# Copies, unit order and warm-up at the start of a hashed attention with a maxout FFN on one Trainium2 core

## The chip, the cores and the metric

The kernel runs on one NeuronCore of a Trainium2 chip. The core has TensorE (PE, matrix products; PEld is its loading of weights), VectorE (DVE), ScalarE (ACT), GpSimd (POOL) and SyncE (SP). The last three also issue DMAs here. The metric is the device time of one execution in microseconds, lower is better. The kernel before took 299.92 us, the median of three runs (297.75 to 301.09).

## The reference

Attention over 4 batches, 8 heads, 768 positions, 64 dimensions. A query sees only the keys of its own hash bucket, six bits from the signs of a projection. The output goes through a maxout layer.

```python
q_bits = (einsum('bhsd,dk->bhsk', q, proj) > 0)      # 6 bits; k_bits alike
mask   = q_bucket[:, :, :, None] == k_bucket[:, :, None, :]
scores = where(mask, scale * q @ k.T, -1e9)
attn   = exp(scores - max); attn = attn / (sum(attn) + 1e-9)
x      = (attn @ v) as (3072, 512)
h      = maximum(maximum(x @ w1, x @ w2), x @ w3)     # 512 -> 768
out    = h @ w_out                                    # 768 -> 512
```

## The kernel before

Heads are worked in 16 pairs. For each pair q and k are loaded as they lie, transposed on TensorE (`tgroup`, L150: one side and one head each, three transposes) and copied out of PSUM to the fp32 tile `T2` (L158, L160). The tile `S` is what the scores read: per side, head and position parity it has 64 rows of data in bf16 and six rows of hash bits as plus or minus one half, so that one product of 70 rows gives score and bit agreement together. `S` is filled from three sides:

- the even copy (`even`, L217): GpSimd copies the lower 64 rows of `T2`, both sides and heads at once
- the odd copies (`odd`, L221): one for k, one for q, from the upper 64 rows; pair 1 has them on VectorE, pairs 8 to 15 on ScalarE; in pairs 2 to 7 the transposes' own step writes the odd rows straight from PSUM (L166, L168)
- the hash (`hashes`, L205): four products with the projection, VectorE makes bits of their signs (L208), and four small DMAs put them into `S` (L214); in pair 1 head 0's two are issued by SyncE, head 1's two by GpSimd

Pair 0 has a start of its own with finer steps (L191, L196).

The unit of work is one pair, one half of the queries (384), two key blocks and one head: 12 units a pair, 192 in all. A unit is two score products (L304) and one exp on ScalarE (L307) into one of 14 `AT` tiles; there are two PSUM buffers for scores. `units` says in which order the key blocks and heads of a half come: by key blocks (both heads of a block, then the next block), or by head (three blocks of head 0, then three of head 1).

The order of all instructions is written out by one loop over the units, and each engine works its own in that order. In iteration u the loop issues, in this order: weight loads at fixed units (on GpSimd), the scores of unit u+1, due steps of the normalization, one waiting late step (`late`), then in some slots either a transpose group of a later pair or, once four groups are through, its hash (`do_hash`). The first group of a pair also issues the loads of q and k of the pair two ahead, on GpSimd. `do_hash` runs the steps that the pair wants in front of the hash, then the hash, and puts those for behind it on `late`, from which one is taken in each iteration.

When a half is complete, `values` multiplies it with v (L328, 24 products) and sums its rows (L342, 12 products), VectorE takes both out of PSUM (L350 to L353), and the reciprocal goes by a DMA round trip (L374 to L388). In some halves the first 16 of the 24 value products come earlier, at slot 4 of the half's six units (`values_part`), since by key blocks the first four chunks of both heads are then there. From unit 61 on, the FFN of the batch before (L246 to L276) fills TensorE between the units; the last batch's FFN is the end of the kernel.

Ahead of everything, TensorE multiplies a tile of zeros several times (L400), while the first loads are on their way.

The loop's lines about the late step and the early values part:

```python
            if late:
                late.pop(0)()
            slot = u % UPG                       # UPG = 6, UPP = 12
            ...
            if slot == 4 and UPP < u < PAIRS_AT: # PAIRS_AT = 60
                values_part(*units[u][0:2], 0, EARLY_CH)
```

Of the kernel before, what the change touches and what calls it, by code (L numbers as in the profile page):

```python
# [17 lines left out]
def kernel(  # L18
# [37 lines left out]
    ODD_LATE, ODD_PSUM = 1, 8  # L56
# [29 lines left out]
    def load_proj():  # L86
        for par in range(2):
            rows = slice(par * D, (par + 1) * D)
            nc.scalar.dma_start(pst[rows, :], proj[:, :])
            nc.vector.tensor_copy(pj[rows, 1 + par, 0:NBITS], pst[rows, :])  # L90
            nc.vector.tensor_copy(pj[rows, 0, par : 2 * NBITS : 2], pst[rows, :])
# [17 lines left out]
    def load(pi, eng):  # L109
        b, jj = divmod(pi, HPAIR)  # L110
        nats = [nat.tile([P, 2, NCH * D], FP32, tag=nm, name=nm) for nm in ("qnat", "knat")]
        for h0, nh in ((0, 1), (1, 1)) if pi == 0 else ((0, 2),):
            for side in (1, 0):
                h = 2 * jj + h0
                eng.dma_start(nats[side][:, h0 : h0 + nh, :],
                                  (q, k)[side][b, h : h + nh].rearrange("h (p c) d -> p h (c d)", p=P))
        natural[pi] = nats

    def load_v(pi, eng):
        b, jj = divmod(pi, HPAIR)  # L120
        vn = vpool.tile([P, 2, NCH * D], FP32, tag="vnat", name="vnat")
        eng.dma_start(vn[:], v[b, 2 * jj : 2 * jj + 2].rearrange("h (p c) d -> p h (c d)", p=P))
        vo = vopool.tile([P, 2, NCH * D], FP16, tag="vo", name="vo")
        vones[pi] = vo
        return lambda: nc.gpsimd.tensor_copy(vo[:], vn[:])
# [7 lines left out]
    def prep_groups(pi):  # L133
        st = {}

        def begin():
            st["T2"] = t2pool.tile([P, 2, 2, HALF], FP32, tag="T2", name="T2")
            st["S"] = spool.tile([KR, 2, 2, 2, HALF], BF16, tag="S", name="S")
            trans[pi] = st["S"]
            if 2 < pi + 2 < NPAIR:  # L140
                load(pi + 2, nc.gpsimd)

        def tgroup(side, hd):
            def go():
                if not st:
                    begin()
                mp = ms_ps.tile([P, 512], FP32, tag="ms", name="mp")
                n = natural[pi][side]
                for i in range(CH2):
                    nc.tensor.transpose(mp[:, i * P : (i + 1) * P], n[:, hd, 2 * i * D : (2 * i + 2) * D], iden[:])  # L150
                o = st["T2"][:, side, hd, :]
                if pi == 0 and (hd, side) != (0, 1):
                    if side == 0:
                        nc.scalar.mul(o, mp[:, 0:HALF], QS)
                    else:
                        nc.scalar.copy(o, mp[:, 0:HALF])
                elif side == 0:
                    nc.vector.tensor_scalar(out=o, in0=mp[:, 0:HALF], scalar1=QS, scalar2=None, op0=AluOp.mult)  # L158
                else:
                    nc.vector.tensor_copy(o, mp[:, 0:HALF])  # L160
                if pi == 0:
                    nc.gpsimd.tensor_copy(st["S"][0:D, side, hd, 0, :], o[0:D])
                elif ODD_LATE < pi < ODD_PSUM:
                    o, i_ = st["S"][0:D, side, hd, 1, :], mp[D : 2 * D, 0:HALF]
                    if side == 0:
                        nc.vector.tensor_scalar(out=o, in0=i_, scalar1=QS, scalar2=None, op0=AluOp.mult)  # L166
                    else:
                        nc.vector.tensor_copy(o, i_)  # L168
            return go
# [49 lines left out]
        def odd(side):  # L219
            copy = nc.scalar.copy if pi > ODD_LATE else nc.vector.tensor_copy  # L220
            return lambda: copy(st["S"][0:D, side, :, 1, :], st["T2"][D : 2 * D, side])  # L221
# [7 lines left out]
                    lambda: bits_first(1, early[2:]), lambda: bits_first(0, ((0, 1, 0, HALF),)),  # L229
                    lambda: bits_first(1, ((0, 1, 0, HALF),))]  # L230
        odds = [odd(1), odd(0)]
        if pi == ODD_LATE:
            return [tgroup(s, h) for h in (0, 1) for s in (1, 0)], hashes, odds + [even], []
        return [tgroup(s, h) for h in (0, 1) for s in (1, 0)], hashes, [even], odds if pi >= ODD_PSUM else []

    def ffn_groups(b):
        xb = xts[b]
# [44 lines left out]
    units = []  # L282
    for pi in range(NPAIR):
        for qh in range(2):
            inner = [(kp, hd) for kp in range(NCH // 2) for hd in range(2)]
            units += [(pi, qh, kp, hd) for kp, hd in (sorted(inner, key=lambda e: e[1]) if pi == 0 else inner)]
    unit_of = {e: u for u, e in enumerate(units)}
    NU = len(units)
    UPB = NU // B
    UPG = NCH  # L290
    UPP = 2 * UPG
# [4 lines left out]
    PAIRS_AT = UPB + UPP  # L296
# [12 lines left out]
    def do_hash():  # L309
        if hash_ready:  # L310
            hs, hv, odds = hash_ready.pop(0)
            for g in odds:
                g()
            hs()
            late.extend(hv)
# [80 lines left out]

    with tc.manual_schedule():
        wm = ms_ps.tile([P, 512], FP32, tag="ms", name="wm")
        for _ in range(9):
            nc.tensor.matmul(wm[:], warm[:, 0:P], warm[:], start=True, stop=True)  # L400
        load(0, nc.sync)
        load_proj()
        load(1, nc.sync)
        cast_v = {0: load_v(0, nc.sync)}
        load(2, nc.sync)
        first = prep_groups(0)
        for g in first:
            g()

        prep, hash_ready, late, ffn, steps = [], [], [], [], []  # L410
        f_credit = 0.0
        for p2 in range(1, NPAIR):
            ts, *hs = prep_groups(p2)
            prep += [(p2, i, g, hs) for i, g in enumerate(ts)]
        for u in range(NU):
            pi = units[u][0]
            b, ub = divmod(u, UPB)
            if u % UPP == 0 and pi + 1 < NPAIR:
                cast_v[pi + 1] = load_v(pi + 1, nc.gpsimd)
            if u == FIRST:  # L420
                cast_v[0]()
            if u % UPP == 10 and pi + 1 < NPAIR:
                cast_v[pi + 1]()
            if u in WEIGHTS_AT:
                nc.gpsimd.dma_start(*weight_parts.pop(0))
            if ub == FFN_AT and b > 0:
                ffn += ffn_groups(b - 1)
            if FIRST < u + 1 < NU:
                scores(u + 1)
            for e in [e for e in steps if e[0] <= u]:  # L430
                e[1]()
                steps.remove(e)
            if late:
                late.pop(0)()
            slot = u % UPG
            if u <= UPG:
                fill = u >= FIRST
            else:
                fill = slot in (2, 3, 5) if u < UPB + FFN_AT else slot in (1, 4)
            if fill:  # L440
                if hash_ready and u < PAIRS_AT:
                    do_hash()
                elif prep and prep[0][0] < pi + AHEAD:
                    _, i, g, hs = prep.pop(0)
                    g()
                    if i == 3:
                        hash_ready.append(hs)
            if slot == 4 and UPP < u < PAIRS_AT:
                values_part(*units[u][0:2], 0, EARLY_CH)
            f_credit = min(f_credit + 0.66, 1.4)  # L450
            while ffn and f_credit > 0:
                c, g, _ = ffn.pop(0)
                g()
                f_credit -= c
            if u >= UPG - 1 + LAG and (u - LAG) % UPG == UPG - 1:
                vp, vq = units[u - LAG][0:2]
                single = vp * UPP < PAIRS_AT or vp % HPAIR == HPAIR - 1
                if single or vq == 1:
                    steps += [(u + n, g) for n, g in values(vp, (vq,) if single else (0, 1),
                                                            EARLY_CH if (vp, vq) in started else 0)]  # L460
                    if u >= PAIRS_AT and vq == 1:
                        do_hash()

        steps = [(n - NU, g) for n, g in steps]
        steps += values(NPAIR - 1, (1,))
        steps.sort(key=lambda e: e[0])
        at = 0
        for c, g, _ in ffn + ffn_groups(B - 1):
            while steps and steps[0][0] <= at:
                steps.pop(0)[1]()  # L470
            g()
            at += c
# [30 lines left out]
```

## Time and profile before

| what | value |
|---|---|
| median of three runs | 299.92 us |
| the profiled execution | 300.85 us |
| its span, first to last instruction | 299.1 us |
| mean granted TensorE clock | 0.988 |
| PE, DVE, ACT, POOL busy | 288.8, 190.3, 194.6, 139.8 us |
| one exp (L307) | 904 ns, 192 of them |
| the even copy (L217) | 1477 ns, 15 of them |
| data moved | 35.90 MB, 120 GB/s mean |

Busy time is per engine and the engines work beside each other. The granted clock is the share of full speed at which TensorE was let run. A row of busy tenths cuts the span in 40 slices of 7.5 us; 9 stands for 90% and more.

### The profile page before, as it was taken

The page shows a single profiled execution, that of the slowest core. Times are in us where ns is not written, and L with a number is a line of the kernel's source. Part 1 is how long each engine was busy: PE and PEld are TensorE (multiplying, and loading weights), DVE is VectorE, ACT ScalarE, POOL GpSimd, SP SyncE. Part 2 cuts the span into 40 slices and gives each one's busy share as a digit, 9 for nine tenths or more (in the row PEclk, how much of TensorE's full clock was granted, in tenths as well). Part 3 has the DMA queues.
Part 4 walks back from the last instruction along what each step waited for, and adds up shares of the span by engine and source line. Part 5 has one row for each costly group of instructions (what it writes and reads, how often), then busy time and mean ns, then how long its engine had stood idle before and what let it go on. Part 6 is the DMA issues. An engine that isn't in the chain of part 4 may idle for free.

```text
span 299.1 us, 6790 instructions
## 1 busy us (share of the span) xinstructions
PE 288.8 (97%) x2593; PEld 162.6 (54%) x2593; DVE 190.3 (64%) x419; ACT 194.6 (65%) x238; POOL 139.8 (47%) x187
## 2 busy tenths in 40 slices
PE   8879999899999999999999999999999999999994
PEld 3444444444566556565566556665655555555551
DVE  2873688877877367663777467663766266758480
ACT  3764888988584966879586966879596957110202
POOL 2762769888874718184723808082700702220000
PEclk9995999999999999999999999999999999999999
DMA  7885088767593442618050452414111211230202
GB/s 211 263 196 154 13 235 184 152 191 212 138 256 104 147 142 66 209 33 278 20 161 30 124 177 59 109 33 160 33 56 37 96 51 46 80 132 2 105 0 106
DMA packets 20277, 35.90 MB, mean 120 GB/s; under 512 B 6081, under 2 KB 12485, under 8 KB 20245
## 3 DMA queue, kind: packets, MB, share of 16 engines
q0 software_dynamic: 8992, 19.81, 24.9%
q1 hardware_dynamic: 10948, 15.52, 16.7%
q8 instruction: 20, 0.33, 0.5%
q10 hardware_dynamic: 304, 0.13, 0.2%
q14 instruction: 13, 0.10, 0.1%
HBM read 31.46 MB, written 6.39 MB: 127 GB/s over the span
## 4 chain that ended last, share of the span: by engine, by line
PE 90%; DMA 3%; ACT 2%; POOL 2%; DVE 1%; issue 1%; SPq 0%; ACTq 0%; POOLq 0%
PE l L246 31%; PE sc L304 21%; PE av L328 11%; PE l L262 10%; PE mp L150 6%; PE sm L342 5%; PE bp L205 4%; DMA rb<-rd 2%; ACT AT L307 2%; PE wm L400 1%; PE bp L191 1%; DMA rd<-rr 1%; POOL S L217 1%; POOL S L214 0%; POOL xT L388 0%
## 5 line engine op out<-in xcount | busy, mean ns | idle before, releaser
L307 ACT ACTIVATE AT<-sc,bias_t 128x768 f16<-128x768 f32 x192 | 168.1, 904 | 59.8 <-PE sc L304 55.1
L246 PE MATMUL l<-xT,w_sb 128*128 128x384 f16 x576 | 110.2, 326 | 0.1
L304 PE MATMUL sc<-S 70*128 70x384 bf16 x384 | 93.7, 330 | 5.1 <-ACT AT L307 3.0
L246 PEld LDWEIGHTS <-w_sb 128*128 128x128 f16 x576 | 55.8, 97 | 35.6 <-issue 0.6
L214 POOL DMA_DIRECT2D S<-bits x58 | 32.9, 570 | 88.3 <-DVE bits L208 58.2
L253 DVE TENSOR_TENSOR ht<-ht,l 128x384 f16<-128x384 f16 x96 | 53.0, 552 | 19.3 <-PE l L246 14.3
L304 PEld LDWEIGHTS <-S 70*128 70x128 bf16 x384 | 34.6, 98 | 45.9 <-issue 21.4
L388 POOL TENSOR_TENSOR xT<-avs,rb 128x384 f16<-128x384 f32 x32 | 31.5, 999 | 34.0 <-DMA rb<-rd 29.4
L251 DVE CAST ht<-l 128x384 f16<-128x384 f32 x48 | 26.6, 553 | 26.2 <-PE l L246 25.0
L328 PE MATMUL av<-AT,vo 128*32 128x385 f16 x768 | 40.1, 335 | 0.0
L262 PE MATMUL l<-wout_sb,ht 128*128 128x512 f16 x144 | 36.5, 379 | 0.0
L276 ACT COPY osb<-l 128x512 f32<-128x512 f32 x23 | 13.5, 585 | 35.0 <-PE l L262 28.4
L328 PEld LDWEIGHTS <-vo 128*32 128x32 f16 x768 | 18.4, 97 | 17.8 <-issue 10.9
L160 DVE COPY T<-mp 128x384 f32<-128x384 f32 x31 | 17.0, 549 | 16.5 <-PE mp L150 13.7
L158 DVE TENSOR_SCALAR T<-mp 128x384 f32<-128x384 f32 x30 | 16.6, 552 | 14.0 <-PE mp L150 12.6
L217 POOL CAST S<-T 64x1536 bf16<-64x1536 f32 x15 | 22.2, 1477 | 0.0
L342 PE MATMUL sm<-AT,ones 128*32 128x384 f16 x384 | 21.9, 331 | 0.0
L262 PEld LDWEIGHTS <-ht 128*128 128x128 f16 x144 | 14.0, 97 | 12.7
L351 DVE TENSOR_SCALAR avs<-av,sv 128x384 f32<-128x384 f32 x32 | 19.8, 618 | 1.6
L353 DVE TENSOR_SCALAR ys<-sm 128x384 f32<-128x384 f32 x32 | 17.5, 548 | 0.1
L150 PE MATMUL mp<-iden,knat 128*128 128x128 f32 x96 | 16.3, 279 | 0.0
L150 PE MATMUL mp<-iden,qnat 128*128 128x128 f32 x96 | 16.0, 275 | 0.0
(45 smaller groups left out, 182.6 us busy)
## 6 DMA issues: line engine op xcount, KB each, us to landing
out_dram<-osb SPq DMA_DIRECT2D x23, 256.0 KB
vnat<-in_v_dram POOLq DMA_DIRECT2D x15, 384.0 KB, 4.9
knat<-in_k_dram POOLq DMA_DIRECT2D x13, 384.0 KB, 4.4
qnat<-in_q_dram POOLq DMA_DIRECT2D x13, 384.0 KB, 5.1
rb<-rd SPq DMA_DIRECT2D x24, 192.0 KB
w_sb<-in_moe_w_dram POOLq DMA_DIRECT2D x12, 192.0 KB, 4.4
rb<-rd SPq DMA_DIRECT2D x16, 96.0 KB
S<-bits POOLq DMA_DIRECT2D x58, 9.0 KB, 2.3
```

What stands on the lines that cost most here:

```text
L150: nc.tensor.transpose(mp[:, i * P : (i + 1) * P], n[:, hd, 2 * i * D : (2 * i + 2) * D], iden[:])
L214: eng.dma_start(st["S"][D:KR, side, hd, :, :], bits[p0 : p0 + 2 * NBITS, :])
L217: nc.gpsimd.tensor_copy(st["S"][0:D, :, :, 0, :], st["T2"][0:D])
L246: nc.tensor.matmul(ps[:, 0:HALF], w_sb[wi][:, jc, fb * P : (fb + 1) * P], xb[:, jc, hf * HALF : (hf + 1) * HALF], start=(jc == 0), stop=(j ...
L251: nc.vector.tensor_copy(hts[fb][:], ps[:, 0:HALF])
L253: nc.vector.tensor_tensor(out=hts[fb][:], in0=hts[fb][:], in1=ps[:, 0:HALF], op=AluOp.max)
L262: nc.tensor.matmul(st2["l2"][:, 0:DM], hts[fb][:, tb * P : (tb + 1) * P], wout_sb[:, fb, :], start=(fb == 0), stop=(fb == NFB - 1))
L304: nc.tensor.matmul(sc[:, j, 0:HALF], th[0:KR, 1, hd, j, kp * P : (kp + 1) * P], th[0:KR, 0, hd, qh, :], start=True, stop=True)
L307: nc.scalar.activation(at[:, :, 0:HALF], sc[:, :, 0:HALF], ActFn.Exp, bias=bias_t[:], scale=SCALE)
L328: nc.tensor.matmul(av[p0 : p0 + 32, 0 : HALF + 1], vones[pi][:, hd, d0 : d0 + 32], at[:, c % 2, 0 : HALF + 1], start=(c == 0), stop=(c == ...
L342: nc.tensor.matmul(sm[32 * t : 32 * t + 32, 0:HALF], ones[:, :], at_of(qh, hd, c)[:, c % 2, 0:HALF], start=(s == 0), stop=(s == CH2 - 1))
L388: return lambda: nc.gpsimd.tensor_mul(xt[:, jj, (q0 + i) * HALF : (q0 + i + 1) * HALF], avs[:, q0 + i, :], rb[:, i, :])
```

## The change

Four edits. In pair 1 the two odd copies run in front of the hash and only the even copy is a late step; before, the late steps of pair 1 were odd, odd, even. The units of pair 1's first half come by head, and those of pair 0's second half by key blocks. With that, the early values part is issued also in pair 0's second half (unit 10) and no longer in pair 1's first half (unit 16). The warm-up has eight products, not nine.

```diff
         odds = [odd(1), odd(0)]
-        if pi == ODD_LATE:
-            return [tgroup(s, h) for h in (0, 1) for s in (1, 0)], hashes, odds + [even], []
-        return [tgroup(s, h) for h in (0, 1) for s in (1, 0)], hashes, [even], odds if pi >= ODD_PSUM else []
+        return [tgroup(s, h) for h in (0, 1) for s in (1, 0)], hashes, [even], odds if pi == ODD_LATE or pi >= ODD_PSUM else []
...
-            units += [(pi, qh, kp, hd) for kp, hd in (sorted(inner, key=lambda e: e[1]) if pi == 0 else inner)]
+            units += [(pi, qh, kp, hd) for kp, hd in (sorted(inner, key=lambda e: e[1]) if pi <= ODD_LATE and qh == 0 else inner)]
...
-        for _ in range(9):
+        for _ in range(8):
             nc.tensor.matmul(wm[:], warm[:, 0:P], warm[:], start=True, stop=True)
...
-            if slot == 4 and UPP < u < PAIRS_AT:
+            if slot == 4 and UPG < u < PAIRS_AT and u // UPG != 2:
                 values_part(*units[u][0:2], 0, EARLY_CH)
```

## The prediction

> **What bounds the kernel now.** I read the page first: busy shares, then the clock row, then the longest waits of TensorE.
>
> ```profile
> PE 288.8 (97%) x2593; PEld 162.6 (54%) x2593; DVE 190.3 (64%) x419; ACT 194.6 (65%) x238; POOL 139.8 (47%) x187
> ...
> PE   8879999899999999999999999999999999999994
> ...
> PEclk9995999999999999999999999999999999999999
> ```
>
> TensorE is busy for 288.8 of 299.1 us, and the row of busy tenths stays at 9 from the ninth slice on. So whatever TensorE gains early arrives at the end. The clock row has one blemish: its fourth slice (22.4 to 29.9 us) reads 5. The second view is the list of TensorE's waits (total us, times, longest).
>
> ```profile
> PE sc L304 <- ACT AT L307: 3.0, 7, 0.7
> PE sc L304 <- POOL S L217: 1.8, 1, 1.8
> ```
>
> One wait of 1.8 us on GpSimd's even copy (L217) stands out. The third view is the chain of work that ended last, around that wait (start, us, what):
>
> ```profile
> 16.69 0.57 DVE bits L208
> 17.26 0.28 issue
> 17.54 1.08 POOL S L214 x2
> 18.62 0.08 issue
> 18.70 0.50 POOL w_sb L425
> 19.21 0.42 issue
> 19.62 0.75 POOL knat L115
> 20.38 0.33 POOL qnat L115
> 20.70 0.35 issue
> 21.06 1.51 POOL S L217
> 22.57 0.05 issue
> 22.62 0.82 PE sc L304 x2
> ```
>
> The even copy needs nothing later than 15.74 us, when VectorE ended the last T2 copy of pair 1. Yet GpSimd starts it at 21.06, because it first waits for the bits (until 17.54), issues two bit DMAs, a weight load and both loads of pair 4. The first scores of pair 1 (unit 12) follow 50 ns after the copy. TensorE's last product before them ended at 20.81 (20.33 + 0.48, scores of unit 11).
>
> The fourth view cuts the time at the clock's own steps (us, then busy us and counts of PE, PEld, DVE, ACT and POOL, then granted clock, DMA share, GB/s):
>
> ```profile
> 15.66:19.08 3.42, 3.42 (x51) 2.43 (x51) 2.00 (x6) 1.49 (x3) 1.54 (x3) 1.00 1.00 219
> 19.08:22.49 3.41, 1.40 (x9) 0.65 (x6) 3.04 (x6) 2.78 (x4) 3.41 (x5) 1.00 0.66 135
> 22.49:25.90 3.41, 3.28 (x23) 1.71 (x27) 1.11 (x2) 1.80 (x2) 2.05 (x4) 0.50 0.83 236
> 25.90:29.31 3.41, 3.41 (x30) 1.69 (x23) 1.34 (x3) 0.72 (x1) 0.00 (x0) 0.50 0.43 99
> 29.31:32.72 3.41, 3.41 (x35) 1.35 (x34) 1.68 (x3) 2.67 (x4) 0.71 (x2) 1.00 0.02 4
> ```
>
> The clock is at half from 22.49 to 29.31, that is 6.82 us, right after a stretch of 3.41 us in which TensorE worked only 1.40. So the wait costs twice: 1.81 us of standing still, and a half clock behind it.
>
> **The change, part by part.**
>
> *Even copy in front of the loads.* It is now the first late step (unit 7), ahead of the weight load and the two loads of unit 8. GpSimd reaches it after the two bit DMAs: 17.54 + 1.17 = 18.71, plus 0.18 from the next part; with 1.50 us it ends at 20.4 in place of 22.56. What it is moved past slips: weight load 0.59 to 0.93, knat 0.75 and qnat 0.74 now start 1.5 to 1.7 us later. Cover: pair 4 is transposed from unit 27 on, some 15 us later, a load of such size lands 4.4 to 5.1 us after issue, and GpSimd then stood idle for 7.47 us before the bits of pair 2. I cost it at nothing. Without that cover it would be the 1.5 us.
>
> *Odd copies in front of the hash.* Two VectorE copies of 0.556 us leave 18.95 to 19.98 and go behind the last T2 copy: 15.74 + 1.11 = 16.85. The bits started at 16.69, so they are 0.16 to 0.18 us late, and so are the four bit DMAs behind them. Queued behind the bits on VectorE are sv, avs and ys of pair 0; sv waited for TensorE until 17.66, with 0.41 us idle before it, so nothing there moves. Do the bits come in time? GpSimd's two are listed at 3.0 to 3.1 us to landing, so 20.6 and 21.2 before, 21.4 at the latest now. SyncE's two have no landing row. The packet records of the trace show 24 packets of 768 bytes on queue q1 from 18.87 to 19.95, so about 20.2 now. Bounds for a scores wait here: 0, and 1.8 us if they took the 4.9 us of a vnat load (18.5 + 4.9 against 21.6). I take 0, which is nearest to the rows of the same DMAs.
>
> *By head in pair 1, by key blocks in pair 0.* No product is added. Sixteen value products (0.77 us in the chain at 31.54) leave unit 16 and go to unit 10, just behind the scores of unit 11, where TensorE stood still: 20.81 + 0.77 = 21.58. Their exps are units 6 to 9, the last of them ended at 20.3. By head, units 12 to 14 need only head 0, whose bits SyncE brings. The price: at unit 18 the second half of the values comes in one piece, 0.77 + 0.44 + 0.49 = 1.7 us, with two exps (start to start 0.79 us) to feed ScalarE meanwhile. ScalarE may idle a microsecond there; the trace has such an idle before (1.93 us ahead of 18.58), with TensorE busy throughout. Bounds 0 to 0.4; I take it into the bubbles below.
>
> *What TensorE then does from 20.81 on.* Full-speed pieces from the chain: eight scores at 0.43 (3.44), three transpose groups at 0.33 (1.0), the hash 0.78, two halves of values at 1.7 (3.4). Sum 8.6 us, so 29.4. Before, the same work ended at 34.33: 4.9 us. What is late next is ScalarE: two score buffers, so scores u wait for exp u-2. I walked the units with 0.90 us for an exp: the waits come at units 16, 18 and 19, together 0.2 to 0.6 us. I take 0.4, so **4.5 us** come off. Check from the other side: 1.81 us of wait plus half of the 6.69 us worked at half clock is 5.16, less bubbles and ScalarE's pace.
>
> *Eight warm-up products.* At 0.43 us from one to the next, the transposes of pair 0 can start at 4.58, not 5.01. The weights of the first transpose were being loaded at 4.58 with no DMA named as their releaser, and the packet records show 418 packets of 1536 bytes started by 4.5, where each of pair 0's loads has 128, so three of its four loads are under way or there. Of the 0.43 us part is lost, because the clock still opens at 5.42 and 0.84 us of transposes then run at half: k of head 0 ends near 5.44, not 5.71. All of the start up to 18 us hangs on that chain. Bounds 0 and 0.43; I take **0.25**.
>
> The Trainium skill, "TensorE: Matmul & The Clock Gate", Part 1, says the gate judges free-running windows of 3413 ns; this trace agrees (6.82 us is two of them). The same page, "Why this matters for your kernels", warns only of idle gaps above about 3 us. By that rule a wait of 1.81 us would not have closed the gate, and the sum would hold the wait alone; that is the fourth rival below. The trace speaks against the rule: 1.81 us and 0.34 us idle in one such window, and half clock from its end on.
>
> *Sum.* The profiled execution took 300.85 us (span 299.1 and 1.75 around it). 300.85 - 4.5 - 0.25 = **296.1 us**. The median shown is 299.92, 0.9 below the profiled one, and the runs span 297.75 to 301.09; a run of 3 us less is what one without the half clock would give (3.35). Such a run would gain only the wait and the warm-up, again about 296. So I keep 296.1 against 299.92, that is 1.3% less.
>
> **The rivals.**
>
> *The clock opens later at the start* (0.11). Before, the stretch 2.01 to 5.42 (one window before the opening) held 3.0 us of warm-up products and 0.4 of transposes. Now it holds 2.6 and 0.8. For it: in 22.49 to 25.90 TensorE stood still only 0.13 us, and the clock did not open at its end; that stretch holds 0.64 us of transposes. Against it: one window sufficed at the start. Price: one more window at half clock, 3.41/2 = 1.7 us, so 297.8.
> The skill's same page, Part 4, says that transposes do not count as busy in the same way; no row here isolates that.
>
> *Slower than before* (0.03). The same mechanism kept up: the clock stays at half from 5.42 on, window after window, because the early stage (8 to 15 us) is full of short waits. At 1.7 us a window, it takes three (to 15.66) to eat 4.75 us, and five (to 22.5) to end at 304.6. Against: half-speed work fills windows better.
>
> *The bits take the even copy's place* (0.06). If the wait was put down to the copy but head 0's bits landed at 22.5 too, or land as late as a vnat load, TensorE stands still for 0.9 to 1.8 us and the clock may close again (3.35): 297.0 to 301.3. Against: the packets at 19.95.
>
> *The clock falls all the same* (0.05). If the fall has nothing to do with the wait, only 1.81 us and the warm-up go: 298.8. Against: the 41% window right before it.
>
> *ScalarE bounds the stretch* (0.07). If unit 18's long piece starves it for a full microsecond that is paid, 297.1.
>
> **How the numbers follow.** My forecast has 0.68, with its own range 295.2 to 296.9 (the terms' bounds: 4.3 to 4.9, and 0 to 0.43; the runs' scatter beside it). The range for 8 in 10 goes down to 294.6, since a median may fall on runs whose clock opens early, and up to 298.6 to take in the late opening and ScalarE. About 1% (3 us) is what a measurement of this kernel can tell from no change: 296.9 is that limit. Forecast mostly below it, half of the ScalarE case below it: faster 0.68. Late opening, falling clock, bits and the rest: same 0.29. Slower 0.03.
>
> **What would show it.** In the profile after: no wait of scores on L217; the even copy starting near 18.6 (18.9 less the warm-up's 0.25), the scores of unit 12 near 21.3 to 21.6; sixteen value products between the scores of units 11 and 12; no 5 in the clock row between 20 and 30 us; the scores of unit 20 near 29.6, not 34.3; from there to the end the same length as before. Wrong would be: a half-clock stretch beyond 5.5 us, scores of unit 12 waiting for a DMA, or a shift of 4.5 us at unit 20 that is given back before the FFN starts.

## The result, and the profile after

The changed kernel takes 296.58 us (median of six runs, 296.21 to 296.79). The kernel before, run beside it, took 300.17 (six runs, 297.75 to 301.16). The ratio is 0.989 with a 95% interval of 0.985 to 0.994: about 1.1% faster, and the interval excludes no change. The forecast was 296.1. The profiled execution of the changed kernel took 296.58 us with a span of 294.5; before, 300.85 and 299.1.

The page of the changed kernel, the same rows as before (busy shares, busy tenths, granted clock in 40 slices):

```profile
PE 284.7 (97%) x2592; PEld 160.8 (55%) x2592; DVE 190.1 (65%) x419; ACT 194.4 (66%) x238; POOL 139.5 (47%) x187
...
PE   7898999999999999999999999999999999999994
...
PEclk9999999999999999999999999999999999999999
```

The 5 in the clock row is gone. TensorE is busy 4.1 us less: some 3.3 of it is half of the 6.69 us that it had worked at half clock, the rest is the product left out and a shorter start at half clock in this execution. Its waits in the changed kernel (total us, times, longest):

```profile
PE sc L302 <- ACT AT L305: 3.8, 9, 0.7
PE wm L398 <- DVE warm L79: 1.2, 1, 1.2
PE mp L150 <- DMA knat<-in_k_dram: 0.6, 1, 0.6
PE sc L302 <- DVE S L196: 0.3, 1, 0.3
```

There is no wait for the even copy (L217). ScalarE's share rose from 3.0 to 3.8, and one wait is new: the transposes of pair 0's second head for their k. The timelines of GpSimd and TensorE around the old wait (start, us, engine, line):

```profile
17.40 1.17 POOL L214 DMA_DIRECT2D S<-bits  x2 [3.40 <-DVE bits L208]
18.56 1.48 POOL L217 CAST S<-T 64x1536 bf16<-64x1536 f32 x1
19.98 0.58 POOL L423 DMA_DIRECT2D w_sb<-in_moe_w_dram  x1
```
```profile
20.18 0.48 PE L302 MATMUL sc<-S 70*128 70x384 bf16 x2
20.59 0.84 PE L326 MATMUL av<-AT,vo 128*32 128x385 f16 x16
21.37 0.50 PE L302 MATMUL sc<-S 70*128 70x384 bf16 x2
...
29.69 0.82 PE L302 MATMUL sc<-S 70*128 70x384 bf16 x4
```

The copy follows the bit DMAs and ends at 20.04, before the weight load. Sixteen value products stand between the scores of unit 11 (20.18) and unit 12 (21.37), with no idle time. The scores of unit 20 begin at 29.69. In the kernel before they began at 34.26:

```profile
34.26 0.82 PE L304 MATMUL sc<-S 70*128 70x384 bf16 x4
```

That is 4.57 us, and the spans differ by 4.6: what was won by unit 20 arrives at the end. The windows that showed the fall of the clock, in the changed kernel:

```profile
15.66:19.08 3.42, 3.39 (x51) 2.40 (x50) 2.67 (x6) 1.49 (x3) 1.68 (x3) 1.00 0.96 183
19.08:22.49 3.41, 3.10 (x34) 1.69 (x37) 2.49 (x5) 3.21 (x5) 3.41 (x5) 1.00 0.43 57
22.49:25.90 3.41, 3.01 (x38) 1.42 (x37) 3.13 (x7) 3.02 (x5) 1.56 (x3) 1.00 1.01 344
25.90:29.31 3.41, 3.06 (x45) 1.65 (x45) 1.67 (x3) 3.05 (x4) 2.18 (x4) 1.00 0.47 90
```

TensorE works 3.10 of 3.41 us where it worked 1.40, and the clock stays whole.

### The profile page after: what moved, and what is told of

It reads as the page before. It is cut to its first block, busy times and chain, and to the rows that moved or that the text cites. A ratio compares the mean times of both kernels' runs of the same rounds, so it can differ in the third digit from the quotient of the medians.

```text
span 294.5 us, 6788 instructions
## 1 busy us (share of the span) xinstructions
PE 284.7 (97%) x2592; PEld 160.8 (55%) x2592; DVE 190.1 (65%) x419; ACT 194.4 (66%) x238; POOL 139.5 (47%) x187
## 4 chain that ended last, share of the span: by engine, by line
PE 92%; ACT 3%; DVE 1%; DMA 1%; issue 1%; SPq 0%; ACTq 0%
PE l L244 31%; PE sc L302 22%; PE av L326 12%; PE l L260 11%; PE mp L150 6%; PE sm L340 5%; PE bp L205 4%; ACT AT L305 3%; DMA knat<-in_k_dram 1%; PE bp L191 1%; SPq L115 0%; DVE avs L349 0%; DVE S L168 0%; DVE S L196 0%; DVE S L166 0%
## 5 line engine op out<-in xcount | busy, mean ns | idle before, releaser
L302 PE MATMUL sc<-S 70*128 70x384 bf16 x384 | 92.2, 326 | 4.0 <-ACT AT L305 3.8
L326 PE MATMUL av<-AT,vo 128*32 128x385 f16 x768 | 39.1, 329 | 0.0
L217 POOL CAST S<-T 64x1536 bf16<-64x1536 f32 x15 | 22.1, 1475 | 0.0
```

The lines of the kernel that those rows point to most:

```text
L217: nc.gpsimd.tensor_copy(st["S"][0:D, :, :, 0, :], st["T2"][0:D])
L302: nc.tensor.matmul(sc[:, j, 0:HALF], th[0:KR, 1, hd, j, kp * P : (kp + 1) * P], th[0:KR, 0, hd, qh, :], start=True, stop=True)
L326: nc.tensor.matmul(av[p0 : p0 + 32, 0 : HALF + 1], vones[pi][:, hd, d0 : d0 + 32], at[:, c % 2, 0 : HALF + 1], start=(c == 0), stop=(c == ...
```

## The experiments

Each time is a median; ratios are to the kernel before on the same chip (300.4 to 300.6 us). The theory: the even copy behind the loads made TensorE stand still; that closed its clock (let it fall to half speed); the change removes both. The rivals ask whether the order of the units, the odd copies, the warm-up or the bits do it.

### The parts alone

**The copies alone.** The kernel before with this edit only:

```diff
-        if pi == ODD_LATE:
-            return [...], hashes, odds + [even], []
-        return [...], hashes, [even], odds if pi >= ODD_PSUM else []
+        return [...], hashes, [even], odds if pi == ODD_LATE or pi >= ODD_PSUM else []
```

> The kernel before with the copies' edit alone: odd copies in front of the hash, the even copy the first late step. Theory (the even copy behind the loads was the whole stall): the even copy ends near 20.2 us, scores of unit 12 start near 21.1 us, no half clock after 5.5 us, median 296.7 us. Rival (the order by head is needed too, since head 1's bits land late): scores of unit 13 wait for a DMA by about 1 us, 297.5 to 299 us.

Measured 296.93 us, ratio 0.988 (0.986 to 0.990). The copies bring all or nearly all of the gain. In the profiled execution the scores of unit 12 wait 0.31 us, for ScalarE, and no scores wait for a bit DMA. Two of the twelve executions, though, have a mean granted clock of 0.991 and 0.988, and took 298.39 and 300.73; none of the six of the changed kernel is below 0.997, and none of the twelve of the two kernels nearest to it (by key blocks and nine products, both below). Whether the values at unit 10 keep that from happening is suggested by this and not settled.

**The order and the early values alone.** The even copy stays behind the loads:

```diff
-(sorted(inner, key=lambda e: e[1]) if pi == 0 else inner)
+(sorted(inner, key=lambda e: e[1]) if pi <= ODD_LATE and qh == 0 else inner)
...
-            if slot == 4 and UPP < u < PAIRS_AT:
+            if slot == 4 and UPG < u < PAIRS_AT and u // UPG != 2:
```

> The kernel before with the unit order and the early values part alone; the even copy still behind the loads. Theory: the copy still ends at 22.56 us, the values at unit 10 fill 0.77 us of the wait, TensorE still stands 1.0 us before the scores of unit 12; 60% busy in such a stretch: if the clock holds, 297.7 us, if it falls, 300 us. Rival (the order by itself removes the stall): 296.6 us.

Measured 298.08 us, ratio 0.9925 (0.9902 to 0.9948). The trace has the wait that was foreseen:

```profile
PE sc L304 <- POOL S L217: 1.0, 1, 1.0
```

The values fill 0.77 us of it, 1.0 is left, and all ten executions have a mean clock of 0.998 or more. So a wait of 1.0 us did not close the clock here, where one of 1.8 mostly does: without touching the copy, this part alone gets two thirds of the gain. The parts overlap; they don't add up.

**Eight warm-up products alone.**

```diff
-        for _ in range(9):
+        for _ in range(8):
```

> The kernel before with eight warm-up products, not nine. Theory (the transposes of head 1 wait for the data, so only 0.1 to 0.2 us are won): 300.0 us median, with runs near 297.8 and near 300 to 301 as in the kernel before. Rival (the clock opens a window later): 1.7 us slower, 301.5 us or more.

Measured 299.85 us, ratio 0.998 (0.9956 to 1.0005): no difference that this can tell, and no sign of a later opening of the clock: it opened at 4.4 us in the profiled execution, at 5.4 in the one of before.

**Nine products in the changed kernel.**

```diff
-        for _ in range(8):
+        for _ in range(9):
```

> The changed kernel with nine warm-up products. Theory: the start is 0.14 us later, 296.7 us. Rival (my term in the prediction): 0.25 us or more, 296.85 us.

Measured 296.83 us (296.35 to 297.38). Between theory and rival there is 0.15 us, less than the scatter of either kernel; the two runs together say only that the product is worth some tenths at most.

### Standing still, and the clock

**The wait filled.** Eight products of zeros, whose result nobody reads, go where TensorE stood in the kernel before; the copy stays late:

```diff
+            if u == 10:
+                fillp = av_ps.tile([P, 512], FP32, tag="av", name="fillp")
+                for _ in range(8):
+                    nc.tensor.matmul(fillp[:], warm[:, 0:P], warm[:], start=True, stop=True)
```

> The kernel before with eight products of zeros (1.73 us) between the scores of unit 11 and of unit 12, where TensorE stood still; their result is not read. The even copy stays late. Theory (the wait costs about 1.3 us by itself and the half clock behind it some 3): the clock stays at full speed, all runs near 297.8 us, none near 300 to 301. Rival (the fall of the clock has nothing to do with TensorE standing still): runs spread from 297.8 to 301 as before, median 300.

Measured 298.44 us, ratio 0.994 (0.992 to 0.996); all twelve executions have a clock of 0.997 or more. Nothing useful was added and nothing made earlier, and 2 us went. The profiled execution shows the scores of unit 12 where they were, right behind the filling:

```profile
20.68 0.49 PE L304 MATMUL sc<-S 70*128 70x384 bf16 x2
21.01 1.89 PE L453 MATMUL fillp<-warm 128*128 128x512 f16 x8
22.97 0.50 PE L304 MATMUL sc<-S 70*128 70x384 bf16 x2
```

The rival falls: the clock fell because TensorE stood still. The median lies 0.6 above what I expected. The clock first opened at 6.28 us in this execution and at 5.42 in the one shown of before, which may be part of that; the rest was not traced.

**The wait put back.** The changed kernel with pair 1's even copy done three times:

```diff
-            nc.gpsimd.tensor_copy(st["S"][0:D, :, :, 0, :], st["T2"][0:D])
+            for _ in range(3 if pi == ODD_LATE else 1):
+                nc.gpsimd.tensor_copy(st["S"][0:D, :, :, 0, :], st["T2"][0:D])
```

> The changed kernel with pair 1's even copy done three times over, so that it ends near 23.0 us and not 20.0; same data. Theory (a stop of TensorE closes the clock): scores of unit 12 wait some 1.6 us, the clock is at half for 6.8 us in some or all executions, runs near 298 without it and near 300.5 with it, median above 299.5. Rival (the fall of the clock in the kernel before had another cause): the wait alone, 298 us in all runs.

Measured 298.47 us, twelve executions. The wait came as made:

```profile
PE sc L303 <- POOL S L218: 1.7, 1, 1.7
```

Eight executions have a clock of 0.997 or more and took 297.74 to 298.71; four have 0.982 to 0.991 and took 300.23 to 302.23. So the wait alone costs some 1.6 us, and the fall of the clock, where it comes, two or more on top. I expected it more often than in one of three.

Why it is rarer here stays open. The sixteen value products stand between this wait and the one of 0.34 us ahead of unit 10, so that a stretch of 3.41 us holds at most 1.7 us of standing still, against 2.1 in the kernel before. But that does not settle it. The clock's steps in a trace lie whole multiples of 3.41 us apart (in the kernel before at 5.42, 22.49 and 29.31), and a wait lies differently between them in each execution. These are stretches between such steps, the first two from the run with eight warm-up products alone, the last from this run, counted on from its opening at 4.33:

```profile
18.04:21.45 3.41, 2.09 (x13) 1.20 (x11) 3.34 (x8) 3.22 (x4) 3.41 (x5) 1.00 0.77 122
21.45:24.86 3.41, 2.59 (x15) 1.37 (x19) 1.47 (x3) 1.41 (x3) 2.74 (x4) 0.50 0.83 250
21.40:24.81 3.41, 1.85 (x27) 1.11 (x27) 0.97 (x2) 1.44 (x3) 3.37 (x4) 1.00 0.22 9
```

In the run with eight products alone the clock fell at 21.45, when the wait (20.46 to 22.27) had lasted 0.99 us and TensorE had worked 2.09 of the 3.41 us. In this run TensorE worked only 1.85 us of its stretch, with the wait at its front, and the clock held. So neither the length of the wait nor how full a stretch is decides alone, and the runs here do not give the rule.

**How often before?** Over the 67 executions of the kernel before that ran beside the first eleven kernels, the mean granted clock sorts the times:

| mean granted clock | executions | median us |
|---|---|---|
| 0.997 | 5 | 297.82 |
| 0.994 | 6 | 299.86 |
| 0.991 to 0.992 | 22 | 300.25 |
| 0.986 to 0.989 | 34 | 300.86 |

With a span of 299 us, 0.994 is some 3.6 us at half clock, and 0.988 some 7.2. The mean also holds up to some 1.7 us at the very end, behind the last product, where the clock falls too (in the profiled execution of the copies alone from 293.76 us on); that alone makes the 0.997 of that execution, and with one stretch of 3.41 us it makes 0.991 to 0.992. So, as the mean clock tells it, the clock fell in 62 of 67, for one or two stretches of 3.41 us, at 2.0 to 3.0 us. Where it fell is seen in the profiled executions only. An execution without a fall lies 1.2 us above the changed kernel: that is the wait itself, with the warm-up product.

**Four warm-up products** in the changed kernel (`range(8)` to `range(4)`):

> The changed kernel with four warm-up products. Theory (what counts is how full TensorE is in a stretch of 3.41 us): TensorE stands from 2.9 to 4.2 us, the clock opens at least one such stretch later, half clock until 8 us or beyond, 1.5 to 4 us slower, 298 to 300.5 us, with a spread between runs. Rival (the number of products does not matter as long as the data come at 4.4): 296.6 us.

Measured 298.26 us (296.96 to 298.64): 1.7 us slower. TensorE's timeline, where three transposes take 0.49 us at full clock and 0.85 to 0.88 at half:

```profile
3.29 0.87 PE L150 MATMUL mp<-iden,knat 128*128 128x128 f32 x3 [0.22 <-DMA knat<-in_k_dram]
3.96 0.85 PE L150 MATMUL mp<-iden,qnat 128*128 128x128 f32 x3
5.38 0.88 PE L150 MATMUL mp<-iden,knat 128*128 128x128 f32 x3 [0.57 <-DMA knat<-in_k_dram]
6.18 2.77 PE L191 MATMUL bp<-T,pj 128*32 128x384 f32 x8
```

The clock's record begins at full speed at 10.3 us here, at 4.2 in the changed kernel. So the mechanism of my first rival, a later opening, is real: it came with four products, and in no profiled execution with eight or nine did the clock open after 7.1 us. Numbers between four and eight were not tried. The first transposes began at 3.29, when the first k was there; head 1's k was waited for until 5.38 all the same.

### What the odd copies and the order by head buy

**Pair 1's first half by key blocks**, in the changed kernel:

```diff
-(sorted(inner, key=lambda e: e[1]) if pi <= ODD_LATE and qh == 0 else inner)
+(sorted(inner, key=lambda e: e[1]) if pi == 0 and qh == 0 else inner)
...
-            if slot == 4 and UPG < u < PAIRS_AT and u // UPG != 2:
+            if slot == 4 and UPG < u < PAIRS_AT:
```

> The changed kernel with pair 1's first half by key blocks again, with its early values part at unit 16. Theory (the order by head does nothing for the wait, and its long piece of values at unit 18 costs ScalarE a microsecond that TensorE does not feel): 296.4 to 296.7 us. Rival 1 (the order by head shields against late bits of head 1): scores of unit 13 wait for a DMA, 297.3 us or more. Rival 2 (the long piece is paid): 295.9 us.

Measured 296.60 us, the same as the changed kernel. ScalarE's idle microsecond at unit 18 is not paid, and the order by head buys nothing here. But this execution's chain holds something else:

```profile
17.59 0.43 SPq L214
18.02 0.06 issue
18.08 3.73 DMA S<-bits
21.81 0.14 issue
21.95 0.49 PE sc L302 x2
```

The scores of unit 12 waited 0.60 us for a bit DMA. Unit 12 is head 0 in either order, and its bits come by SyncE, so the order has no part in it. The last of the 24 packets of 768 bytes is recorded at 20.47, and TensorE was released at 21.81: 1.3 us later. In the prediction I took the last packet for the landing.

**The odd copies behind the hash**, behind the even copy:

```diff
-hashes, [even], odds if pi == ODD_LATE or pi >= ODD_PSUM else []
+hashes, [even] + (odds if pi == ODD_LATE else []), odds if pi >= ODD_PSUM else []
```

> The changed kernel with the odd copies of pair 1 behind the hash again, now behind the even copy (units 8 and 9 at the latest). Theory (only the even copy's place behind the loads cost anything): VectorE ends the odd copies near 20 us, before the scores of unit 12 at 21.4, so 296.6 us, within 0.3. Rival (the odd copies had to go in front too): scores of unit 12 wait for VectorE, 297.2 us or more.

Measured 297.89 us (297.73 to 298.44), clock 0.997 or more: 1.3 us slower than the changed kernel. My theory falls, and so does the rival as I put it, for no scores wait for VectorE. VectorE's timeline:

```profile
18.33 0.55 DVE L351 TENSOR_SCALAR ys<-sm 128x384 f32<-128x384 f32 x1
18.89 2.17 DVE L221 CAST S<-T 64x768 bf16<-64x768 f32 x1
20.99 0.54 DVE L160 COPY T<-mp 128x384 f32<-128x384 f32 x1
```

and GpSimd's beside it:

```profile
18.64 1.48 POOL L217 CAST S<-T 64x1536 bf16<-64x1536 f32 x1
20.06 0.58 POOL L423 DMA_DIRECT2D w_sb<-in_moe_w_dram  x1
```

The odd copy takes 2.17 us where it takes 0.55 alone. It started while GpSimd's copy ran, and ended 0.94 us after it. VectorE's queue is then 1.6 us late; the last T2 copy of pair 2 ends at 26.66, and the hash of pair 2 waits for it, with two of its products gone ahead:

```profile
26.71 0.85 PE L205 MATMUL bp<-T,pj 128*32 128x384 f32 x6 [0.44 <-DVE T L158]
```

The chain of this execution runs over VectorE from 18.89 to 26.66, and the scores of unit 20 begin at 31.04, 1.35 us later than in the changed kernel, which is all of the difference. VectorE's copies out of PSUM are not stretched so: in the changed kernel they took 0.56 us each (19.09, 19.66) beside the same GpSimd copy. The Trainium skill, "SBUF — State Buffer", "Who interferes with whom", has one port pair that VectorE and GpSimd lock against each other for a whole instruction; these rows fit that in part. Behind GpSimd's copy, which ended at 20.12, the 0.55 us of the odd copy would end at 20.67, and not at 21.06; the other 0.4 us are not explained.

**The same on ScalarE**, on top of the edit before it:

```diff
-            copy = nc.scalar.copy if pi > ODD_LATE else nc.vector.tensor_copy
+            copy = nc.scalar.copy
```

> The odd copies of pair 1 behind the even copy, as in the run with the odd copies late, but done by ScalarE. With VectorE, the first of them took 2.17 us beside GpSimd's even copy, in place of 0.55, and the hash of pair 2 waited for VectorE. Theory (VectorE's copy is held by GpSimd's copy, ScalarE's would not be): the copies take about 0.9 us each beside the even copy, VectorE is not late for the hash of pair 2, ScalarE's exps slip by 1 to 2 us; 296.8 to 297.8 us. Rival (any engine reading T2 beside GpSimd is held): the ScalarE copy takes 2 us or more, and the time is 298.5 us or above.

Measured 298.55 us. The copies take 0.83 us each and VectorE is on time (the bits of pair 2 follow their hash at once), as the theory has it. The first ran at 20.34, when GpSimd's even copy was over at 20.23, so it says little; the second, at 22.12, ran beside GpSimd's cast of v (22.17, 0.87 us), and neither took longer, while in the run before that cast beside VectorE's second odd copy took 1.19. So ScalarE's copies were not held, but the time is the rival's: the price on ScalarE was larger than I gave, and TensorE's waits for it rose from 3.8 to 5.6 us. One of the twelve executions has a clock of 0.987 and took 300.80.

### Another order of the slots

**Slots 1, 2 and 5, and slots 1, 3 and 5**, in the changed kernel, for what is left of TensorE's waits:

```diff
-                fill = slot in (2, 3, 5) if u < UPB + FFN_AT else slot in (1, 4)
+                fill = slot in (1, 2, 5) if u < UPB + FFN_AT else slot in (1, 4)
```

> The changed kernel with transposes and hashes in slots 1, 2 and 5 of a half, not 2, 3 and 5, from unit 7 to 60. What is left of TensorE's waits are some eight of 0.4 us, each before the third scores behind a half's values. Theory (TensorE's order can cover ScalarE's pace there): each such wait falls to 0.2 us or less, 1.5 us off, 295.1 us. Rival (ScalarE's pace bounds the stretch whatever the order): 296.6 us.

> As the run before it, with slots 1, 3 and 5. Theory: one wait of 0.2 us in place of 0.4 in each half, 295.1 us. Rival: 296.6 us.

Measured 300.29 and 297.89 us, both slower than the changed kernel, with a clock of 0.997 or more in all executions but one. The waits for ScalarE did not shrink (3.9 and 4.7 us against 3.8): with 1, 3 and 5 the old waits stay and more come (twelve, not nine). With 1, 2 and 5 there are new ones, 1.6 us of the FFN for the normalized x and 0.5 us of a hash for VectorE. Theory and rival are both wrong here; what makes up the rest of the 3.7 us was not followed up. No kernel tried beats the changed one.

## Why the prediction was right, and where it was off

The result lies 0.5 us above the forecast and inside its own range.

- **The wait and the half clock behind it**: right in mechanism. The filled wait, the wait put back and the 67 executions show each of the two by itself. One reading was loose: of the 1.81 us, 1.68 lay in the stretch that ended at 22.49, where the clock fell. The stretch from 20.8 us to unit 20 was sized at 4.5; with the start's 0.14 taken off, 4.57 leaves 4.4. That it comes so close is in part luck: TensorE waited 0.75 us for ScalarE there (0.40 at unit 16, 0.35 at unit 19), above the bound of 0.6 that I gave and the 0.4 that I took, and the work itself took less than the 8.6 us that I added up, some 8.35 of the 9.10 us in the chain.
- **How the two share it**: the check sum gave 1.81 and 3.35, less bubbles. Over the executions, the fall costs 2.0 to 3.0 us and the wait with the warm-up 1.2. Both are smaller than their plain size. That ScalarE's pace would have held TensorE for a part of either fits the 0.75 us above, but no run isolates it.
- **The even copy**: forecast to end at 20.4 less 0.25, so 20.15; it ended at 20.04. The scores of unit 12 came at 21.37 (21.3 to 21.6 forecast), those of unit 20 at 29.69 (29.6).
- **The loads that slipped**: nothing in the trace waits for them, as assumed.
- **Eight warm-up products**: sized 0.25; the two traces give 0.14 (scores of unit 8 at 17.90, not 18.04). No run shows even that for sure: with nine products in the changed kernel those scores began at 17.83, so the scatter of the opening is as large as the term. The step that failed is the reading of the packet records, 418 packets by 4.5 us as three loads "under way or there". The transposes of head 1's k waited 0.55 us for the third load and began at 5.76, before at 5.87. A started packet is not yet a landed load; whether the packets were also spread over later loads is not shown.
- **The bits**: costed at 0 with more than a microsecond to spare, "about 20.2 now". The same misreading, of a packet for a landing: in one execution (pair 1 by key blocks) they were the last to come, at 21.81. The term held in the profiled execution of the changed kernel, but its margin is not the 1.4 us that I worked out: with the last packet there at 19.77, the same 1.3 us give an estimate of 21.1 against the scores at 21.37. The Trainium skill, "DMA: Bandwidth & Descriptors", "Anatomy of one DMA", puts most of the fixed cost of a DMA on GpSimd's path behind its last byte; this DMA is on SyncE's path, and its 1.3 us behind the last packet are of the same kind.
- **The odd copies**: I saw only their cost, bits 0.16 us late, and not what they avoid. Left behind the even copy they cost 1.3 us. Where they stood in the kernel before, at 18.95 and beside no GpSimd copy, they took 0.556 us each; it is the even copy moved forward that would have met them there. So this step of the change was priced as a small cost where it avoids a loss.
- **The order by head**: costed at about nothing, and measured so (296.60 against 296.58).
- **The base**: I forecast from the profiled execution and expected that one without half clock would end at about 296 too. Five such executions at 297.82 bear out that they exist; against them the changed kernel gains 1.2 us, less than the wait and the warm-up that I counted (2.06).
- **The size**: 4.27 us between the profiled executions against a sum of 4.75. Of the missing 0.48, 0.11 is the warm-up by these two traces, and 0.33 lies outside the spans (1.75 us around it before, 2.08 after).

## What to carry to other kernels

Where one engine is busy all the way, look for the single wait in its list and then at the clock right behind it: the stop may cost twice. A wait that can't be removed can still be filled: filling it with products of zeros alone brought 2.0 of the 3.6 us. Before a copy from SBUF to SBUF is put on VectorE, look whether GpSimd copies there at the same time; and take the release, never the last packet, for the end of a DMA.

## What the runs showed of the hardware that I had not expected

- One wait of 1.8 us, with 0.34 us idle ahead of it, went with a clock at half for one or two stretches of 3.41 us in 62 of 67 executions (by the mean clock); a wait of 1.7 us in 4 of 12, one of 1.0 us in none of 10. The length of the wait alone is not the rule: in the run with eight warm-up products alone the clock fell 0.99 us into it.
- The clock can open behind a stretch that is mostly transposes. In the run with the copies alone, the clock's record begins at full speed at 7.04 us, and the 3.41 us before that held 1.4 us of warm-up products and about 2 of transposes:

```profile
1.20 4.02 PE L398 MATMUL wm<-warm 128*128 128x512 f16 x9 [1.20 <-DVE warm L79]
5.01 0.85 PE L150 MATMUL mp<-iden,knat 128*128 128x128 f32 x3
5.65 0.85 PE L150 MATMUL mp<-iden,qnat 128*128 128x128 f32 x3
6.29 0.85 PE L150 MATMUL mp<-iden,knat 128*128 128x128 f32 x3
```

  This speaks against the premise of my first rival, that transposes count for less. The run with four warm-up products speaks for it: from 3.45 to 6.87 us TensorE was busy for 2.85 us, some 2.2 of them transposes, and the clock stayed at half for another 3.41 us. How transposes count stays open. With eight or nine products the opening lay between 3.9 and 7.0 us, from one execution to the next.
- A fp32 to bf16 copy on VectorE took 2.17 us in place of 0.55 when it started beside a GpSimd copy of 1.48 us.
- From the last recorded packet of a 9 KB DMA to the release of the engine that waits for it, 1.3 us passed.
